# BigBird attention and a low-rank mixer: where the one-hot mask rows and the identity come from, and the order of the first copies

## Chip, cores, metric

The kernel runs on one core of one Trainium2 chip. The metric is the device time of one execution in microseconds (us). Lower is better. A version is timed in several executions, and their median is compared.

The engines have these names in the profile: PE is TensorE (matmul), PEld its weight loads, DVE is VectorE, ACT is ScalarE, POOL is GpSimd, SP is SyncE, which here only issues transfers. A "q" behind the name (SPq, ACTq) is the engine's issue of transfers or its sequencer.

## The reference

Inputs: q, k, v of 4 batches x 8 heads x 768 tokens x 64 channels, a table of 3 sampled key blocks for each of the 24 query blocks (a block has 32 tokens), and the weights U (768x32), V (32x768), w1 (512x2048) and w2 (2048x512) of a mixer. All but the table are float32.

```python
scores = scale * np.matmul(q, k.transpose(0, 1, 3, 2))
mask = np.abs(blk_i - blk_j) <= 1
mask = mask | (blk_i == 0) | (blk_j == 0) | (blk_i == n_blocks - 1) | (blk_j == n_blocks - 1)
for qb in range(n_blocks):
    for kb in sampled_blocks[qb]:
        mask[qb * block:(qb + 1) * block, kb * block:(kb + 1) * block] = True
scores = np.where(mask, scores, -1000000000.0)
scores = scores - np.max(scores, axis=-1, keepdims=True)
attn = np.exp(scores)
attn = attn / (np.sum(attn, axis=-1, keepdims=True) + 1e-09)
attn_out = np.matmul(attn, v)
x = np.ascontiguousarray(attn_out.transpose(0, 2, 1, 3)).reshape(B, S, H * D)
h = x.transpose(0, 2, 1) @ U @ V
u = x + h.transpose(0, 2, 1)
out = u + np.maximum(u @ w_ch1, 0.0) @ w_ch2
```

## The kernel before

**Pairs of heads.** The 32 heads are worked as 16 pairs, four pairs to a batch. For each pair q and k are turned (channels to partitions), scores are made as keys x queries in PSUM, exponentials are taken from there on ScalarE, and the exponentials are the weights of the products with v. In the first batch (pairs 0 to 3) the mask is put into the scores themselves: a head uses 64 partitions for its channels (`drows`), and 24 of the other 64 partitions (`mrows`) for the mask. On the query side (`qres`) these rows hold a one-hot row for each block, on the key side (`kres`) the bias (0 or -240) of each key and block. One matmul over 128 partitions then gives score plus bias. Head 0 of a pair has its channels in partitions 0 to 63 and its mask rows from 64, head 1 the other way round. There are two such sets (`qres[0]`, `kres[0]` and `qres[1]`, `kres[1]`), all four in one tile `res`, used by even and odd pairs. Later batches multiply the exponentials by a mask in SBUF, which `mask_part` (PLAN letter K) makes from `kmask` and the one-hot rows.

**The start (lines 234 to 342).** It is written out by hand, engine by engine. SP issues the loads of q and k of head 0, then the one-hot rows of the first set (`one_hot`, two loads from a constant in memory), then head 1, v and the next pair. ScalarE issues the loads of `small` (a constant of 128 rows with the static mask, the block numbers and the 128x128 identity) and of the table `sb`. VectorE zeroes the unused rows. TensorE does eight matmuls of ones with 512 columns (`keep_warm`, line 272). VectorE casts q of head 0 to float16 (`first_cast`), makes the bias from table and constants (lines 302 to 309), and casts k. The first turns (`first_turn`, line 227) are matmuls of the 64 channels of head 0 with the identity: three to a half of 384 tokens (c), for q (n = 0) and k (n = 1). `first_row` (line 293) copies a half to its rows of the set. `mask_half` (line 279) multiplies the bias by the one-hot rows, into PSUM bank 2 for c = 0 and bank 7 for c = 1, and `mask_row` (line 287) copies 24 rows of it to the mask rows of a head. GpSimd zeroes the second set, writes the column of ones of the v tiles `vts`, casts q and k of head 1, zeroes `Vt` and `kmask` and casts what comes in later. `second_set` copies the mask rows of the first set to the second and to `kmask` by transfers on SP.

**The order behind it.** A string, PLAN (line 448), has a word for each step; the steps are issued in its order, and each engine works on what it is given in that order. A capital letter takes the next step of its kind, a digit behind it is its PSUM bank. S is a score of one block of 128 keys (`score`, line 980), B a score of two (`two_scores`, line 999, three banks from the digit on), e the exponential of the oldest score that has none, Z the turn of q and k of pair 0 for head 1 (`last_turn`, line 352, both heads wide), z its copy (line 359), A a product with v, R the turn of a later pair, K a part of the SBUF mask. It begins:

```
S0 S3 e e S5 B0 e Z7 e S3 z Z6 e z A7 A B0 e R6 S3 t A R5 e A B0 t A K6 e A S3 k v A5 A e K6 k B0 A
```

`begin(i)` runs as the first score of pair i is issued, and issues loads of later pairs (`loads`). S0 uses PSUM banks 0 and 1, S3 banks 3 and 4, S5 banks 5 and 6, B0 banks 0 to 2. The first turns of k are in banks 5 and 6.

## Time and profile before

| what | us |
|---|---|
| three runs | 269.93, 270.38, 272.29 |
| median | 270.38 |
| the profiled execution, whole | 270.01 |
| its span, first to last instruction | 268.2 |
| TensorE at work in the span | 262.4 |
| VectorE | 232.5 |
| ScalarE | 202.7 |
| GpSimd | 72.7 |

The granted TensorE clock is 0.999 in the mean over the span. All times of the trace are counted from the start of the span. Busy times of matmuls hold a modelled drain, so that neighbours overlap in it: the start of the next is the better measure. The profile merges instructions of one line that follow each other into one row, "x8", with the length from the first start to the last end. A row's "[0.22 <-ACT res L287]" says that the engine had been idle for 0.22 us, and what ended that. L293 is line 293 of the listing.

### The profile page before, as it was taken

The numbers are of one execution on the slowest core, as the hardware profiler recorded it, in microseconds if no ns is written. First come the engines' busy times: TensorE is split into PE (matmuls) and PEld (weight loads), VectorE is DVE, ScalarE is ACT, GpSimd is POOL, SyncE is SP. The second block draws the span as 40 slices with busy tenths as digits, with TensorE's granted clock in tenths as the row PEclk, the third lists the DMA queues.
The fourth block names the chain that finished last, engine by engine and source line by source line (L and its number), as shares of the span: only waits on it lengthen the run. The fifth ranks groups of instructions, "written<-read, shape, count | busy, mean of one in ns | idle before, by whom it ended". The sixth has DMA issues, their size and how long they took to land.

```text
span 268.2 us, 7303 instructions
## 1 busy us (share of the span) xinstructions
PE 262.4 (98%) x3006; PEld 182.4 (68%) x3006; DVE 232.5 (87%) x477; ACT 202.7 (76%) x265; POOL 72.7 (27%) x98
## 2 busy tenths in 40 slices
PE   8899999999999999999999999999999999999995
PEld 3677775555577778565666887555667788666884
DVE  5789988988999998868588997688998999999993
ACT  4999998897989667788898857788997944789200
POOL 4669006944462570070606160000000000000000
PEclk9999999999999999999999999999999999999999
DMA  6799997999999999897938997610200116400024
GB/s 192 245 324 263 207 235 123 113 135 144 189 146 133 117 103 111 284 98 89 90 39 67 106 109 139 223 34 13 51 0 2 42 42 117 159 2 0 2 98 137
DMA packets 88720, 31.66 MB, mean 118 GB/s; under 512 B 77104, under 2 KB 85840, under 8 KB 88688
## 3 DMA queue, kind: packets, MB, share of 16 engines
q0 software_dynamic: 49728, 10.10, 48.4%
q1 hardware_dynamic: 38492, 20.86, 33.6%
q8 instruction: 23, 0.38, 0.6%
q10 hardware_dynamic: 468, 0.26, 0.4%
q14 instruction: 9, 0.07, 0.1%
HBM read 27.67 MB, written 6.29 MB: 127 GB/s over the span
## 4 chain that ended last, share of the span: by engine, by line
PE 73%; DMA 12%; DVE 7%; ACT 2%; POOL 2%; issue 1%; SPq 0%; DVEq 0%; POOLq 0%; ACTq 0%
PE ps L760 32%; PE ps L685 17%; DMA w2t<-in_moe_w_ch_dram 9%; PE ps L414 9%; PE ps L1030 7%; DMA vld<-in_v_dram 2%; PE ps L999 2%; ACT est L1007 2%; PE ps L980 1%; DVE est L1045 1%; PE ps L272 1%; DMA qpl<-stqld 1%; PE ps L665 1%; DVE xf L551 1%; DVE res L969 1%
## 5 line engine op out<-in xcount | busy, mean ns | idle before, releaser
L1039 ACT ACTIVATE est<-ps 128x1536 f16<-128x1536 f32 x72 | 100.6, 1450 | 18.8 <-PE ps L1030 18.7
L685 PE MATMUL ps<-uT,w1t 128*128 128x384 f16 x384 | 70.2, 326 | 0.0
L1045 DVE TENSOR_TENSOR est<-est,mask 128x1440 f16<-128x1440 f16 x72 | 63.4, 903 | 0.6 <-ACT est L1039 0.2
L685 PEld LDWEIGHTS <-w1t 128*128 128x128 f16 x384 | 35.6, 97 | 26.6 <-issue 6.8
L414 PEld LDWEIGHTS <-est 128*128 128x128 f16 x1152 | 40.4, 97 | 7.0 <-issue 3.3
L414 PE MATMUL ps<-vt,est 128*128 128x65 f16 x1152 | 43.3, 193 | 0.2 <-DVE xf L551 0.2
L760 PEld LDWEIGHTS <-hid 128*128 128x128 f16 x358 | 34.0, 98 | 6.6 <-issue 1.6
L697 ACT ACTIVATE hid<-ps 128x384 f16<-128x384 f32 x63 | 29.7, 496 | 4.8 <-PE ps L685 4.3
L1030 PE MATMUL ps<-qpl,kpl 64*128 64x512 f16 (+1 forms) x288 | 31.7, 325 | 0.0
L139 POOL DMA_DIRECT2D stqld<-in_q_dram x20 | 16.3, 820 | 55.9 <-DMA qpl<-stqld 54.4
L760 PE MATMUL ps<-w2t,hid 128*128 128x256 f16 x238 | 31.1, 273 | 0.0
L879 DVE TENSOR_TENSOR xf<-xf,ps 128x256 f32<-128x256 f32 x63 | 25.4, 416 | 4.1 <-PE ps L760 3.7
L699 DVE TENSOR_SCALAR hid<-ps 128x384 f16<-128x384 f32 x33 | 18.3, 555 | 8.7 <-PE ps L685 8.0
L760 PEld LDWEIGHTS <-sums 128*128 128x128 f16 x216 | 20.1, 98 | 4.4 <-issue 1.0
L989 ACT ACTIVATE est<-ps 128x768 f16<-128x768 f32 x30 | 22.5, 812 | 0.1
L1030 PEld LDWEIGHTS <-kpl 64*128 64x128 f16 x288 | 12.3, 94 | 14.3 <-issue 9.1
L760 PE MATMUL ps<-res,sums 128*128 128x256 f16 x144 | 19.4, 273 | 0.0
L634 ACT CAST xh<-xf 128x384 f16<-128x384 f32 x24 | 11.0, 510 | 10.0 <-DVE xf L630 10.0
L551 DVE TENSOR_TENSOR xf<-ps,rcp 128x384 f32<-128x384 f32 x32 | 17.7, 554 | 0.8
L139 POOL DMA_DIRECT2D stkld<-in_k_dram x20 | 16.3, 819 | 1.9 <-issue 0.8
L139 POOL DMA_DIRECT2D vt<-in_v_dram x20 | 16.3, 820 | 0.0
L760 PE MATMUL ps<-res,hid 128*128 128x256 f16 x120 | 15.9, 273 | 0.0
(121 smaller groups left out, 339.3 us busy)
## 6 DMA issues: line engine op xcount, KB each, us to landing
out_dram<-xf SPq DMA_DIRECT2D x18, 256.0 KB, 2.4
vld<-in_v_dram SPq DMA_DIRECT2D x6, 384.0 KB, 6.3
w1t<-in_moe_w_ch_dram POOLq DMA_DIRECT2D x4, 512.0 KB, 8.3
w2t<-in_moe_w_ch_dram POOLq DMA_DIRECT2D x4, 512.0 KB, 12.1
qld<-in_q_dram SPq DMA_DIRECT2D x5, 384.0 KB, 3.7
kld<-in_k_dram SPq DMA_DIRECT2D x5, 384.0 KB
stqld<-in_q_dram POOLq DMA_DIRECT2D x20, 96.0 KB, 3.9
stkld<-in_k_dram POOLq DMA_DIRECT2D x20, 96.0 KB, 4.2
```

What stands on the lines that cost most here:

```text
L139: nc.gpsimd.dma_start(out=dst[:, h], in_=src[b, 2 * hp + h].rearrange("(p t) d -> p t d", t=T),)
L414: nc.tensor.matmul(pav[:, sc, :], est[:, n, sc * P : (sc + 1) * P], vts[b % 2][:, 2 * hp + h, g, 0 : D + 1], start=(g == 0 and sc == 0), s ...
L551: nc.vector.tensor_tensor(out=dst, in0=pav[:, :, 0:D], in1=rcp[:, :, None].broadcast_to([P, T, D]), op=ALU.mult,)
L685: nc.tensor.matmul(pt, w1t[:, cc, jj * P : (jj + 1) * P], bts[b].uT[:, cc, c * HS : (c + 1) * HS], start=(cc == 0), stop=(cc == NCC - 1), ...
L697: nc.scalar.activation(out=dst, in_=pt, func=AF.Relu)
L699: nc.vector.tensor_scalar_max(out=dst, in0=pt, scalar1=0.0)
L760: nc.tensor.matmul(acc[key], lhsT, rhs, start=(first and i == 0), stop=(i == len(pairs_) - 1), skip_group_check=True,)
L879: nc.vector.tensor_add(out=x, in0=x, in1=acc[a, b, tau])
L989: lambda: nc.scalar.activation(out=dst, in_=ps, func=AF.Exp, scale=0.125),
L1030: nc.tensor.matmul(units[h][:, u * S + lo : u * S + hi], kT[drows[h], g * P : (g + 1) * P], qT[drows[h], lo:hi], start=True, stop=True, sk ...
L1039: nc.scalar.activation(out=both[h], in_=units[h].rearrange("p (g n) -> p g n", g=2), func=AF.Exp, scale=0.125,)
L1045: lambda: nc.vector.tensor_mul(out=masked(both[h]), in0=masked(both[h]), in1=masked(mask[:, 2 * j : 2 * j + 2, :]),),
```

## The change

- The identity becomes a constant of its own, `id16`, loaded by SP between q and k of head 0.
- One-hot rows, static mask and block numbers become one constant of 32 rows (`hot`), loaded by ScalarE's queue. The load goes to partitions 0 to 31 of `res`, from the query rows of head 1 of the first set on, and 50 elements into the next: the one-hot rows thus land where head 1 of the first set needs them, and the constants in rows of the second set that are filled later.
- Head 0 of the first set gets its one-hot rows (and the zeros below) by a copy on ScalarE, the second set by two transfers inside SBUF (`second_hot`). The four loads of `one_hot` are gone. VectorE zeroes 32 rows of head 1 in the place of 64 of each head.
- The first turns take both heads of the staged tile as weights (128 columns for 64); head 1's half is zeroed by GpSimd before. Their output has 128 partitions, of which 64 are read.
- There are seven warming matmuls of 512 columns and one of 256 in the place of eight.
- The copies are dealt out anew: `first_row(1, 0)` is all VectorE's, `first_row(1, 1)` ScalarE's. The second `mask_half`, and the mask copies but for the first, go to a step of their own, `late_masks`, behind the first score (W7 in PLAN; bank 7), with `second_set` and the load of V.
- GpSimd writes the ones of `vts` and zeroes `kmask` behind its casts of head 1; it zeroes `Ut` (which VectorE did) and `Vt` beside the cast of U. It zeroes only the rows of the second set that no copy fills.
- The loads of pair 2 are issued at the first score of pair 1 in the place of pair 0.

```diff
--- before.py
+++ after.py
@@ -64,14 +64,14 @@
     ).astype(np.float32)
     cols = np.arange(S)
     blk = ((cols % P) * T + cols // P) // BLK
-    ohT_np = (blk[None, :] == ii[:, None]).astype(np.float16)
-    small_np = np.zeros((P, NB + 1 + P // 2), np.float32)
-    small_np[:NB, :NB] = (ms_np - 1.0) * -MASK_BIAS
-    small_np[:NB, NB] = ii
-    small_np[:, NB + 1 :] = np.eye(P, dtype=np.float16).view(np.float32)
-
-    small_dr = nc.inline_tensor(small_np, name="small_const")
-    ohT_dr = nc.inline_tensor(ohT_np, name="one_hot_const")
+    NROW = 32
+    hot_np = np.zeros((NROW, S // 2 + NB + 1), np.float32)
+    hot_np[:NB, : S // 2] = (blk[None, :] == ii[:, None]).astype(np.float16).view(np.float32)
+    hot_np[:NB, S // 2 : S // 2 + NB] = (ms_np - 1.0) * -MASK_BIAS
+    hot_np[:NB, S // 2 + NB] = ii
+
+    hot_dr = nc.inline_tensor(hot_np, name="hot_const")
+    id_dr = nc.inline_tensor(np.eye(P, dtype=np.float16), name="identity_const")
 
     consts = ctx.enter_context(tc.tile_pool(name="consts", bufs=1))
     wpool = ctx.enter_context(tc.tile_pool(name="wpool", bufs=1))
@@ -99,10 +99,7 @@
         ring["psc"] += 1
         return PS[:, (0, 3)[ring["psc"] % 2] :][:, 0:2]
 
-    small = consts.tile([P, NB + 1 + P // 2], FP32)
-    ms = small[0:NB, 0:NB]
-    iota = small[0:NB, NB : NB + 1]
-    id16 = small[:, NB + 1 :].bitcast(FP16)
+    id16 = consts.tile([P, P], FP16, name="id16")
     sb = consts.tile([P, NB, 3, 2], I32)
     vts = [consts.tile([P, H, T, DV], FP16, name=f"vt{i}") for i in range(2)]
     NEST = 16
@@ -112,6 +109,9 @@
     res = consts.tile([P, 4, 2, S], FP16, name="res")
     qres = [res[:, i] for i in range(2)]
     kres = [res[:, 2 + i] for i in range(2)]
+    hot = res.rearrange("p a b s -> p (a b s)")[:, S : 2 * S + 2 * NB + 2].bitcast(FP32)
+    ms = hot[0:NB, S // 2 : S // 2 + NB]
+    iota = hot[0:NB, S // 2 + NB :]
     drows = [slice(0, D), slice(D, P)]
     mrows = [slice(D, D + NB), slice(0, NB)]
     hid = consts.tile([P, 2, 16, HS], FP16, name="hid")
@@ -183,22 +183,24 @@
             out=lds[nm][:, h], in_=src[0, h].rearrange("(p t) d -> p t d", t=T)
         )
 
-    def one_hot(i, h):
-        nc.sync.dma_start(out=qres[i][mrows[h], h, :], in_=ohT_dr.ap())
+    def second_hot(h):
+        nc.sync.dma_start(out=qres[1][mrows[h], h, :], in_=qres[0][mrows[h], h, :])
 
     warm = nc.const_aps.tensor(1.0, [P, 512], mybir.dt.bfloat16)
     bias = consts.tile([P, 2, D], FP16)
 
     def second_set():
         for h in range(2):
-            one_hot(1, h)
             nc.sync.dma_start(out=kres[1][mrows[h], h, :], in_=kres[0][mrows[h], h, :])
-        nc.sync.dma_start(out=kmask[mrows[0], :], in_=kres[0][mrows[0], 0, :])
+            if h == 0:
+                nc.sync.dma_start(out=kmask[mrows[0], :], in_=kres[0][mrows[0], 0, :])
 
     def load_mix_u():
         uld = ldpool.tile([P, T, R], FP32, tag="ldu", name="uld", bufs=1)
         nc.sync.dma_start(out=uld, in_=moe_U.rearrange("(p t) r -> p t r", t=T))
+        nc.gpsimd.memset(Ut.bitcast(FP32), 0.0)
         nc.gpsimd.tensor_copy(out=Ut[:, :, 0:R], in_=uld)
+        nc.gpsimd.memset(Vt.bitcast(FP32), 0.0)
 
     def load_mix_v():
         vld = ldpool.tile([P, 2, T, D], FP32, tag="ldv", name="vld")
@@ -225,8 +227,8 @@
         first_out[n, c] = pt
         for j in range(3):
             nc.tensor.matmul(
-                pt[0:D, j * P : (j + 1) * P],
-                sts[0, ("qld", "kld")[n]][:, 3 * c + j, 0],
+                pt[:, j * P : (j + 1) * P],
+                sts[0, ("qld", "kld")[n]][:, 3 * c + j].rearrange("p h d -> p (h d)"),
                 id16,
                 start=(j == 0), stop=(j == 2), skip_group_check=True,
             )
@@ -241,30 +243,31 @@
         }
     ):
         first_load(0, 0, nc.sync)
+        nc.sync.dma_start(out=id16, in_=id_dr.ap())
         first_load(0, 1, nc.sync)
-        nc.scalar.dma_start(out=small, in_=small_dr.ap())
+        nc.scalar.dma_start(out=hot[0:NROW], in_=hot_dr.ap())
         nc.scalar.dma_start(
             out=sb[0:NB].rearrange("k z r w -> k (z r w)"),
             in_=sampled_blocks.bitcast(I32)
             .rearrange("z r -> (z r)")[None, :]
             .broadcast_to([NB, NB * 6]),
         )
-        for h in (1, 0):
-            nc.vector.memset(qres[0][(slice(D, P), slice(0, D))[h], h, :], 0.0)
-            one_hot(0, h)
+        nc.vector.memset(qres[0][NROW:D, 1, :], 0.0)
         nc.vector.memset(bias, 0.0)
         for h in range(2):
-            nc.vector.memset(kres[0][(slice(D, P), slice(0, D))[h], h, :], 0.0)
+            nc.vector.memset(kres[0][drows[1 - h], h, :], 0.0)
         for n in range(2):
             first_load(1, n, nc.sync)
+        for nm in ("qld", "kld"):
+            nc.gpsimd.memset(sts[0, nm][:, :, 1], 0.0)
         for tile_ in (qres[1], kres[1]):
-            nc.gpsimd.memset(tile_.bitcast(FP32), 0.0)
-        for vt in vts:
-            nc.gpsimd.memset(vt[:, :, :, D : D + 1], 1.0)
+            for h in range(2):
+                nc.gpsimd.memset(tile_[drows[1 - h], h, :].bitcast(FP32), 0.0)
         first = consts.tile([P, 1], FP32)
         nc.scalar.activation(
             out=first, in_=nc.const_aps.tensor(1.0, [P, 1], FP32), func=AF.Exp
         )
+        nc.scalar.copy(out=qres[0][drows[1], 0, :], in_=qres[0][drows[0], 1, :])
         pw = psc2()
 
         def keep_warm(n, cols=512):
@@ -273,7 +276,7 @@
                     pw[:, 0, 0:cols], warm[:, 0:P], warm[:, 0:cols], start=True, stop=True
                 )
 
-        pks = [bank(2, [P, HS], FP32), bank(7, [P, HS], FP32)]
+        pks = [bank(2, [P, HS], FP32)]
 
         def mask_half(c):
             nc.tensor.matmul(
@@ -297,7 +300,8 @@
 
         neq = consts.tile([P, NB, 3], FP32)
         a01 = consts.tile([P, NB], FP32)
-        keep_warm(8)
+        keep_warm(7)
+        keep_warm(1, 256)
         first_cast(0, 0, nc.vector.tensor_copy)
         nc.vector.tensor_tensor(
             out=neq[0:NB], in0=sb[0:NB, :, :, 0],
@@ -318,26 +322,30 @@
         first_cast(0, 1, nc.vector.tensor_copy)
         mask_half(0)
         mask_row(0, 0, nc.vector.tensor_copy, 0, P)
-        mask_row(1, 0, nc.scalar.copy)
         first_turn(1, 0)
         first_row(1, 0, nc.vector.tensor_copy, 0, P)
-        first_row(1, 0, nc.scalar.copy, P, HS)
         mask_row(0, 0, nc.vector.tensor_copy, P, HS)
+        first_row(1, 0, nc.vector.tensor_copy, P, HS)
         first_turn(1, 1)
-        first_row(1, 1, nc.vector.tensor_copy)
-        mask_half(1)
-        mask_row(0, 1, nc.vector.tensor_copy)
-        mask_row(1, 1, nc.vector.tensor_copy)
+        first_row(1, 1, nc.scalar.copy)
 
         for n in range(2):
             first_cast(1, n, nc.gpsimd.tensor_copy)
-        for tile_ in (Vt, kmask):
-            nc.gpsimd.memset(tile_.bitcast(FP32), 0.0)
-        nc.vector.memset(Ut, 0.0)
+        for vt in vts:
+            nc.gpsimd.memset(vt[:, :, :, D : D + 1], 1.0)
+        nc.gpsimd.memset(kmask.bitcast(FP32), 0.0)
         load_v(0)
         load_qk(1)
         load_v(1)
         load_mix_u()
+        for h in range(2):
+            second_hot(h)
+
+    def late_masks(n):
+        pks.append(bank(n, [P, HS], FP32))
+        mask_half(1)
+        for h, c in ((0, 1), (1, 0), (1, 1)):
+            mask_row(h, c, nc.vector.tensor_copy)
         second_set()
         load_mix_v()
 
@@ -446,7 +454,7 @@
 
 
     PLAN = """
-    S0 S3 e e S5 B0 e Z7 e S3 z Z6 e z A7 A B0 e R6 S3 t A R5 e A B0 t A K6 e A S3 k v A5 A e K6 k B0 A
+    S0 W7 S3 e e S5 B0 e Z7 e S3 z Z6 e z A7 A B0 e R6 S3 t A R5 e A B0 t A K6 e A S3 k v A5 A e K6 k B0 A
     A e K7 A K6 k S3 k A K7 e v B0 k S3 e M6 e A5 A m R7 A t B0 K6 R3 e k A A t S6 A e v S0 D2 S3 e d A7
     A e A S0 K6 A e S3 k K2 A e S5 k A e v S3 R2 e S5 t S0 e M7 e S3 m D2 e B5 d A0 D1 e A A d A S3 D2 A
     e d K1 S5 k R7 e S3 t A S1 e v A5 A e A S3 S6 e K2 A e A k A S3 v B0 e K7 M6 e k S3 m X5 K7 e A6 Y k
@@ -1073,7 +1081,7 @@
         elif i == HP + 2:
             for c in range(1, 4):
                 nc.sync.dma_start(out=Vt[c * R : (c + 1) * R], in_=Vt[0:R])
-        for m in {0: (0,), 1: (1, 2), 3: (3,), 4: (4,)}.get(i, ()):
+        for m in {1: (0, 1, 2), 3: (3,), 4: (4,)}.get(i, ()):
             loads(m)
 
     def first_scores():
@@ -1122,6 +1130,7 @@
         "E": ((lambda n, i=i, c=c: pairs[i].sum_only(c, n),) for i, c in each(range(XP, HP), (0, 1))),
         "R": ((turn_qk, i, n) for i, n in each(range(1, HP + 1), (0, 1))),
         "Z": ((last_turn, n) for n in range(2)),
+        "W": ((late_masks,) for _ in range(1)),
         "K": ((mask_part, g, c) for g, c in each(range(T), (0, 1))),
         "P": ((lambda n, jj=jj: w1(0, 0, jj, n, range(2)),) for jj in range(NPART)),
         "C": ((lambda jj=jj: w1(0, 0, jj, ccs=(2, 3)),) for jj in range(NPART)),
```

## The prediction

> **What bounds the kernel now.** I read three things in order: the busy shares on the page, the busy time by stage, and the chain of waits through the first 10.4 us, which is all the change touches. First the page and the table by stage (from:to in us, length, then busy time and count of each engine, granted clock, DMA share, GB/s).
>
> ```profile
> PE 262.4 (98%) x3006; PEld 182.4 (68%) x3006; DVE 232.5 (87%) x477; ACT 202.7 (76%) x265; POOL 72.7 (27%) x98
> ```
>
> ```profile
> 0.00:4.00 4.00, 3.22 (x8) 1.02 (x8) 2.12 (x7) 1.49 (x2) 2.08 (x8) 1.00 0.48 133
> 4.00:8.00 4.00, 3.50 (x22) 1.69 (x22) 2.99 (x9) 3.02 (x7) 1.72 (x4) 1.00 0.88 268
> ```
>
> TensorE is idle 5.8 us of the span (268.2 - 262.4), and 0.78 + 0.50 = 1.28 of them lie in the first 8 us; the first 0.78 is the launch. Work behind the start is therefore nearly a queue that begins when the start lets it: what the start gains or loses is moved to the end almost one for one, and little else can be gained. Now the chain there (start, length, work).
>
> ```profile
> 0.78 3.57 PE ps L272 x8
> 4.35 0.47 PE ps L227 x3
> 4.84 0.85 ACT res L293 x2
> 5.69 0.46 ACT res L287
> 6.17 0.42 DVE res L287
> 6.62 0.55 DVE res L293
> 7.21 0.57 DVE res L287
> 7.82 0.82 PE ps L999 x4
> 8.64 0.34 PE ps L352 x6
> 8.98 0.32 PE ps L980 x2
> 9.30 0.35 PE ps L352 x6
> 9.74 0.57 DVE res L359
> 10.36 0.84 PE ps L999 x4
> ```
>
> Eight warming matmuls hold TensorE to 4.35, then come the turns of the first q, two copies and a mask copy on ScalarE, three copies on VectorE, the fused score B0 at 7.82, and the turns of the second heads with a last copy before the second B0 at 10.36. The timeline of the same stretch gives starts and lengths of single operations.
>
> ```profile
> 0.73 1.41 POOL L261 MEMSET res<- 128x768 f32 x2 [0.29 <-POOLq L1168]
> 1.20 0.41 SPq L182 DMA_DIRECT2D kld<-in_k_dram  x1
> 1.65 0.80 SPq L187 DMA_DIRECT2D res<-one_hot_const  x2
> 3.15 0.20 ACT L265 ACTIVATE first<-const-float32-1.0 128x1 f32<-128x1 f32 x1
> 3.47 0.36 DVE L213 CAST stqld<-qld 128x384 f16<-128x384 f32 x1 [0.52 <-DMA qld<-in_q_dram]
> 4.28 0.60 PEld L227 LDWEIGHTS <-stqld 128*64 128x64 f16 x6 [0.84 <-DVE a L306]
> 4.38 0.34 DVE L213 CAST stkld<-kld 128x384 f16<-128x384 f32 x1
> 5.24 0.52 PE L227 MATMUL ps<-small,stkld 128*64 128x128 f16 x6
> 5.35 0.29 DVE L287 CAST res<-ps 24x128 f16<-24x128 f32 x1 [0.62 <-PE ps L279]
> 5.67 0.28 DVE L293 CAST res<-ps 64x128 f16<-64x128 f32 x1
> 6.17 0.42 DVE L287 CAST res<-ps 24x256 f16<-24x256 f32 x1 [0.22 <-ACT res L287]
> 6.54 2.23 ACT L989 ACTIVATE est<-ps 128x768 f16<-128x768 f32 x3
> 6.74 0.81 PE L980 MATMUL ps<-res 128*128 128x384 f16 x4 [0.23 <-DVE res L287]
> 7.21 1.13 DVE L287 CAST res<-ps 24x384 f16<-24x384 f32 x2
> 8.41 0.82 POOL L131 CAST vt<-vld 128x768 f16<-128x768 f32 x1 [0.90 <-DMA vld<-in_v_dram]
> 8.68 1.45 ACT L1007 ACTIVATE est<-ps 128x1536 f16<-128x1536 f32 x1
> 13.89 1.55 POOL L207 CAST Vt<-vld 32x768 f16<-32x768 f32 x1 [0.56 <-DMA vld<-in_moe_V_dram]
> ```
>
> **The change, part by part.**
>
> *Half a warming matmul less.* Eight took 3.57 us, 0.446 each, so TensorE is free 0.22 us sooner. The q cast is done at 3.47 + 0.36 = 3.83, so the turn can use that time.
>
> *Wide turns.* Weights of 128 columns replace weights of 64, the moving side stays 128 columns. The rows of weight loads and matmuls (min/median/max ns) are:
>
> ```profile
> L227 PEld LDWEIGHTS <-stqld x6: 128/175/177, 4.3 to 4.7; 128*64 128x64 f16 x6
> L227 PE MATMUL ps<-small,stqld x6: 234/314/316, 4.3 to 4.8; 128*64 128x128 f16 x6
> L352 PEld LDWEIGHTS <-stqld x6: 96/98/98, 8.3 to 8.7; 128*128 128x128 f16 x6
> L227 PE MATMUL ps<-small,stkld x6: 217/218/243, 5.2 to 5.5; 128*64 128x128 f16 x6
> ```
>
> A wide load at full speed takes 98 ns, and in the chain its turns (8.64, six in 0.34) load ahead of the matmul before. The narrow loads began only at 4.28, as the last warming matmul drained, 0.45 us after their cast. I take a further 0.06 us from loading ahead (between 0 and 0.13, to which the cast's end limits it). The first turn starts 0.28 us sooner, about 4.07 in the chain's times. The Trainium skill, page "TensorE: Matmul & The Clock Gate", section "LDWEIGHTS (loading the stationary operand)", speaks against this: a load costs its columns over 1.2 GHz whatever its rows, so a wide one would be twice a narrow one, 107 against 53 ns, and twelve turns would lose up to 0.6 us if nothing hid it. The rows here say otherwise (98 ns for 128 columns), and the rows decide.
>
> *The constants.* The identity leaves ScalarE's DMA and gets its own on SP, ahead of the k load, whose issue slips by one issue, about 0.4 us (k's here takes 0.41). The mask constants and the one-hot rows come in one load on ScalarE's queue; two one-hot issues (0.80 us) leave SP, so everything behind k on SP goes about 0.4 sooner. In 2.8 to 3.2 us the DMA view has these rows, and the k load its time to landing:
>
> ```profile
> q10 hardware_dynamic: 26, 0.01, 8.3%
> ```
>
> ```profile
> kld<-in_k_dram SPq DMA_DIRECT2D x1, 192.0 KB, 2.9
> ```
>
> The first is ScalarE's queue, which moves its last packets there, so the constants are in by about 3.2 and should be in the new form too. k lands at 1.20 + 2.9 = 4.1 and will at about 4.5; its cast, at 4.38 now, slips to about 4.55 and ends near 4.9, and the k turn that stood at 5.24 can start near 4.95. That is 0.29 sooner, just the lead. The cover here is thin: each tenth by which k lands after 4.55 is lost.
>
> *ScalarE's copy of the one-hot rows.* Nearest row: the three exponentials of 768 columns, 2.23 us, 0.74 each. Behind the first activation (ends 3.35) it ends at 4.1. ScalarE's next work stood at 4.84 and comes at about 4.56. Cost nothing; if the constants came at 4.0, 0.2 us would be lost.
>
> *GpSimd.* Two memsets of the staged tiles (half of res's 0.70 each at most) go ahead of the turns, done by about 1.5. The zeroing of Ut and Vt, some 0.4 us each, now stands between the second v cast and Vt's cast, where GpSimd waited 0.56 for a DMA; the earlier loads give the rest. The ones column and kmask follow the second heads' casts, before v at 8.41, which waited 0.90 for its DMA. Cost nothing; without that cover, 0.3 us of GpSimd time, not on the chain. loads(0) is moved behind the late masks' SP transfers, where those stood before, so no queue order changes there.
>
> *The copies.* This is where the lead is spent. ScalarE loses a mask copy (0.46) and a k copy and gains the last k copy (row L293); VectorE loses that and gains the k copy of 256 columns (0.42, as the mask copy of that width) and a mask copy (0.57), and its wait of 0.22 on ScalarE goes. From starts to starts: the first mask copy 5.35 becomes 5.07, then 0.32, 0.31, 0.45 and 0.45, so the four rows are in by 6.57 where they were by 6.59. The second score, at 6.74, gains 0.02. The three late mask copies at 0.58 each start at 6.60, 7.18 and 7.76 and end at 8.31; the last ended at 7.21 + 1.13 = 8.34. The late mask matmul stands between the first and second score, where TensorE waits anyway.
>
> *What is late next.* The first exponential comes 0.28 sooner (6.26), the second only 0.02 to 0.04, as its scores wait for VectorE; the fourth, B0's, follows the third on ScalarE at 8.66 against 8.68. B0 itself no longer waits at 7.82: three of its matmuls need the first late copy and the fourth the second (bank 2), 7.75, so it ends near 8.15 in place of 8.64. The turn Z7 then waits for the third (bank 7), 8.31, and starts at about 8.37, against 8.48 for its weight-ahead start; the chain has it after B0 at 8.64, so the lead is between 0.11 and 0.27. I take 0.11, the timing of its start. Z7, a score, Z6, the copy and the second B0 follow unchanged: 10.36 becomes 10.25, and the exponential behind it has ScalarE free by then (8.66 + 1.45 = 10.11, then a single one). **Sum: 0.1 us sooner**, with 0.0 and 0.28 as bounds.
>
> **To the time measured.** The profiled execution took 270.01 (span 268.2); less 0.11 is 269.90. The three runs have 269.93, 270.38 and 272.29, median 270.38; less 0.11 is 270.27. The profiled one lies 0.37 under the median, and I take halfway: 270.1.
>
> **The rivals.**
>
> *The clock stays low.* The q turns took 316 ns, the last of them 234, the k turns 218: TensorE's clock rose at about 4.7, after 3.9 us of matmuls without a gap. With half a matmul less a gap can open, if the identity, now behind q on SP, lands after 4.1. If the clock then stays low for another such stretch, the work up to 8.2 us doubles: two mask products and three pairs of scores of 384 columns, B0 and the k turns, by the chain's rows 0.32 a pair and 0.82 for B0, some 2.4 us, less the 0.50 idle: +1.9, so 272.2. Against it: q lands at 3.4, the identity is a sixth of its bytes just behind, and a gap of a tenth is small. Decided by whether TensorE idles by more than a few tenths before 4.7. Chance 0.08. The skill's page named above, Part 1, has the clock wait for a busy window of 3.4 us that runs freely; seven and a half warming matmuls at 0.446 are 3.35, just less, but the turns behind them are matmuls too; the rise after 3.9 us here agrees with such a window and cannot show where it begins.
>
> *No gain.* k lands after 4.8, or VectorE's new copies cost 0.1 more: 270.4 to 270.7. For it: VectorE has no idle time left between 5.1 and 8.3. Chance 0.25.
>
> *More gain.* The lead of the first turn, 0.28, survives, and the earlier loads take up the remaining gaps to 16 us (0.2 or so each): 0.5 to 0.8 sooner, 269.5. Against it: VectorE. Chance 0.14.
>
> *Later transfers collide.* Loads go 0.4 us sooner, and TensorE later works from weights that arrive by DMA; a slip there of 3 us would pass to the end. Nothing in the first 16 us says that it will: 273 and over. Chance 0.04.
>
> The forecast keeps 0.49. The range reaches from 269.2 (more gain, and the 0.3 by which runs differ) to 271.4 (no gain, the same added to the runs above the median), and leaves out the low clock and the collision. Over 1% is 2.7 us, about what a measurement of this kernel can tell from no change; only the collision gets there, and nothing shown saves as much: faster 0.02, within 0.94, slower 0.04.
>
> **What would show it.** Right: the first turn's weight load near 4.0 with q turns at about 315 ns and k turns at 218; the first exponential near 6.25 but the second still near 7.2; VectorE without a gap from 5.1 to 8.3; Z7 near 8.4 and the second B0 near 10.25; from 24 us the same pattern, shifted. Wrong: matmuls of 300 ns behind 5 us (clock), a k cast after 4.8, a ScalarE copy that ends after 4.5, or a shift at 16 us that the end does not have.

## The result and the profile after

| | before | after |
|---|---|---|
| median of 22 executions each, us | 270.38 | 272.12 |
| lowest and highest, us | 269.65, 272.29 | 270.59, 273.86 |
| profiled execution, us (span) | 270.01 (268.2) | 270.59 (268.8) |
| ratio after/before, 95% interval | | 1.0057 (1.0040 to 1.0073) |

The changed kernel is slower by 0.6%, less than the 1% that counts as a change here, but outside the range of the prediction. Two numbers have to be explained: the profiled executions differ by only 0.6 us, the medians by 1.7. Of the 22 times after, 7 lie from 270.59 to 271.48 and 15 from 271.82 up; of those before, 20 lie at 270.94 or below. The profiled execution after is the fastest of its 22, so it shows what the fastest execution loses, and not what is lost most of the time.

The page of after, and its table by stage for the first 8 us (from:to, length, busy time and count of PE, PEld, DVE, ACT, POOL, granted clock, DMA share, GB/s):

```profile
PE 262.0 (97%) x3006; PEld 182.3 (68%) x3006; DVE 232.3 (86%) x476; ACT 203.4 (76%) x265; POOL 74.1 (28%) x103
```

```profile
0.00:4.00 4.00, 3.21 (x10) 1.15 (x11) 1.82 (x7) 2.12 (x3) 2.62 (x10) 1.00 0.46 114
4.00:8.00 4.00, 2.97 (x22) 1.45 (x21) 3.08 (x9) 2.77 (x6) 1.80 (x5) 1.00 0.91 279
```

From 4 to 8 us TensorE now works 2.97 us where it worked 3.50. The timeline of after there (start, length, work, and the idle time before it with what ended it):

```profile
1.21 0.41 SPq L246 DMA_DIRECT2D id<-identity_const  x1
1.66 0.43 SPq L182 DMA_DIRECT2D kld<-in_k_dram  x1
...
3.37 0.83 ACT L270 COPY res<-res 64x768 f16<-64x768 f16 x1
...
3.87 0.35 PEld L229 LDWEIGHTS <-stqld 128*128 128x128 f16 x6 [0.43 <-POOL res L265]
3.90 0.49 PE L229 MATMUL ps<-id,stqld 128*128 128x128 f16 x6
...
4.92 0.36 DVE L215 CAST stkld<-kld 128x384 f16<-128x384 f32 x1 [0.56 <-DMA kld<-in_k_dram]
...
5.43 0.49 PE L229 MATMUL ps<-id,stkld 128*128 128x128 f16 x6 [0.68 <-DVE stkld L215]
...
6.67 2.40 ACT L997 ACTIVATE est<-ps 128x768 f16<-128x768 f32 x3 [0.24 <-PE ps L988]
...
6.99 1.60 DVE L290 CAST res<-ps 24x384 f16<-24x384 f32 x3
...
8.64 0.50 PE L360 MATMUL ps<-id,stqld 128*128 128x128 f16 x6
...
9.79 0.54 PE L422 MATMUL ps<-vt,est 128*128 128x65 f16 x12
...
10.52 0.82 PE L1007 MATMUL ps<-res 128*128 128x512 f16 x4 [0.19 <-DVE res L367]
```

The q turns start 0.4 us sooner than before (weight load 3.87 for 4.28), and at 218 ns a turn they run at full speed at once. Then TensorE stands idle for 0.68 us, because k of head 0 is not there: VectorE itself waits 0.56 for the transfer and casts k at 4.92, where it did at 4.38. The k turns come at 5.43 for 5.24, the second B0 at 10.52 for 10.36. The first product with v starts at 9.79; before it was here:

```profile
9.63 0.54 PE L414 MATMUL ps<-vt,est 128*128 128x65 f16 x12
```

So the start loses 0.16 us. The second loss is far behind the change, at 30 us. The timeline of VectorE and TensorE there, after:

```profile
29.09 0.55 DVE L624 TENSOR_TENSOR xf<-xf,ps 128x384 f32<-128x384 f32 x1
...
29.97 0.48 PE L988 MATMUL ps<-res 128*128 128x384 f16 x2
...
30.09 0.55 DVE L623 TENSOR_TENSOR xh<-xh,ps 128x384 f16<-128x384 f16 x1 [0.45 <-issue]
...
31.16 0.32 PE L947 MATMUL ps<-res,kmask 128*128 128x384 f16 x1 [0.35 <-DVE xf L624]
...
31.98 0.49 PE L988 MATMUL ps<-res 128*128 128x384 f16 x2
```

And the same sum of VectorE and the same two scores of TensorE before:

```profile
29.52 0.56 DVE L615 TENSOR_TENSOR xh<-xh,ps 128x384 f16<-128x384 f16 x1
...
29.81 0.48 PE L980 MATMUL ps<-res 128*128 128x384 f16 x2
...
31.43 0.48 PE L980 MATMUL ps<-res 128*128 128x384 f16 x2
```

VectorE stops for 0.45 us ahead of the third of the low-rank sums (the steps D of PLAN), and nothing that the profile shows is being waited for ("issue"). TensorE waits 0.35 for it. The distance between the kernels, 29.97 - 29.81 = 0.16 ahead of it, is 31.98 - 31.43 = 0.55 behind it. The profiled executions end 0.58 us apart, so these two places are nearly all of that difference. The other 1.2 us of the medians are not in this trace.

### The profile page after: what moved, and what is told of

Same layout as the page of the kernel before. It is cut to its first block, busy times and chain, and to the rows that moved or that the text cites. A ratio compares the mean times of both kernels' runs of the same rounds, so it can differ in the third digit from the quotient of the medians.

```text
span 268.8 us, 7310 instructions
## 1 busy us (share of the span) xinstructions
PE 262.0 (97%) x3006; PEld 182.3 (68%) x3006; DVE 232.3 (86%) x476; ACT 203.4 (76%) x265; POOL 74.1 (28%) x103
## 4 chain that ended last, share of the span: by engine, by line
PE 66%; DMA 10%; DVE 7%; POOL 3%; issue 1%; ACT 1%; DVEq 0%; POOLq 0%; ACTq 0%
PE ps L768 31%; PE ps L693 17%; PE ps L422 7%; PE ps L1038 7%; DMA stqld<-in_q_dram 5%; DMA vt<-in_v_dram 4%; PE ps L988 1%; DVE est L1053 1%; POOL stkld L139 1%; DMA qpl<-stqld 1%; DVE xf L887 1%; POOL stqld L139 1%; DVE sums L863 1%; DVE sums L729 1%; DVE xf L559 1%
```

## The experiments

Each kernel was executed 6 to 12 times and timed against the kernel before on the same chip; ratios are to that, as recorded. They are not the quotients of the medians of all executions (for six warming matmuls these medians, 270.82 and 270.19, give 1.0023). "Lowest" is the distance of its fastest execution from the fastest of the kernel before on that chip.

| kernel | ratio (95% interval) | lowest, us |
|---|---|---|
| after again | 1.0055 (1.0028 to 1.0082) | +0.84 |
| k ahead of the identity | 1.0053 (1.0017 to 1.0090) | +0.78 |
| three matmuls in the gap | 1.0067 (1.0033 to 1.0101) | +1.20 |
| before, 7.5 warming matmuls | 0.9999 (0.9967 to 1.0032) | -0.16 |
| identity on ScalarE's queue | 1.0088 (1.0066 to 1.0110) | +1.64 |
| the same, one more zeroing | 1.0115 (1.0092 to 1.0137) | +2.72 |
| after, one more zeroing | 1.0044 (1.0020 to 1.0067) | +0.59 |
| before, a transfer ahead of k | 1.0043 (1.0014 to 1.0072) | +0.20 |
| after, constants as before | 1.0025 (1.0006 to 1.0044) | +0.65 |
| before, six warming matmuls | 1.0000 (0.9979 to 1.0021) | -0.33 |
| one matmul in the gap | 1.0035 (1.0014 to 1.0056) | +0.96 |
| before, wide turns and 7.5 | 1.0010 (0.9981 to 1.0040) | -0.39 |
| before, two zeroings moved | 0.9977 (0.9951 to 1.0002) | +0.40 |
| constants as before, one more zeroing | 1.0010 (0.9972 to 1.0048) | +0.11 |
| before, four warming matmuls | 1.0048 (1.0019 to 1.0076) | +1.54 |
| identity on GpSimd's queue | 1.0015 (0.9983 to 1.0047) | +0.87 |
| two zeroings moved, again | 1.0001 (0.9986 to 1.0017) | +0.60 |
| its twin with one more | 0.9994 (0.9973 to 1.0015) | +0.45 |

### The changed kernel once more

> The changed kernel, unchanged, for the trace of another of its executions. In the one profiled, k's cast waits for its load until 4.92 us and TensorE is idle for most of 4.7 to 5.4; its 270.59 us is the fastest of 22 runs, whose median is 272.12. Theory K (late k load: the identity's transfer on SP ahead of k holds up the k turns, nothing else): this trace looks like the first, and the ratio to before is 1.002 to 1.004. Theory C (clock: the idle stretch keeps TensorE's clock low for longer in most executions, so that the start costs 1 to 2 us there): matmuls behind 5.4 us take about 0.31 us for 128 columns in place of 0.22, the second fused score starts at 11.5 or later (10.52 in the first trace), ratio 1.005 to 1.007. Theory L (later transfers): the start as in the first trace, the time is lost behind 16 us.

It came out as the first time, 1.0055. Its profiled execution took 271.74 and is one of the slower kind. Its timeline:

```profile
3.93 0.84 PE L229 MATMUL ps<-id,stqld 128*128 128x128 f16 x6
...
5.68 0.80 PE L229 MATMUL ps<-id,stkld 128*128 128x128 f16 x6 [0.48 <-DVE stkld L215]
...
7.72 1.46 PE L988 MATMUL ps<-res 128*128 128x384 f16 x4
...
9.85 0.50 PE L360 MATMUL ps<-id,stqld 128*128 128x128 f16 x6
...
11.01 0.54 PE L422 MATMUL ps<-vt,est 128*128 128x65 f16 x12
```

Six turns last 0.84 and 0.80 where they lasted 0.49, and 0.50 again from 9.85 on. TensorE's clock rose at 9.43 us here; in the first profiled execution it rose at 3.50. (Each trace's record of the granted clock begins at that rise. Ahead of it the column of the tables by stage reads 1.00 though the matmuls are slow, so a first rise is told by the durations of equal matmuls, not by that column.) The first product with v starts at 11.01 for 9.79, 1.22 later, and the execution is 271.74 - 270.59 = 1.15 longer. This is a part of the loss that the first trace doesn't show.

The lateness of k varies too. In the five traces that have the identity ahead of k, its cast starts at 4.92, 5.17, 5.30, 5.33 and 5.50: the first trace is the mildest.

### Half a warming matmul less, alone

```diff
-        keep_warm(8)
+        keep_warm(7)
+        keep_warm(1, 256)
```

> The kernel before with seven and a half warming matmuls in place of eight and nothing else. The prediction: up to 0.2 us faster, ratio 0.999 to 1.000. Theory C with the shorter warming as its cause: ratio 1.003 or more, q turns at 314 ns and k turns no faster.

The ratio is 0.9999 (to 1.0032): no cost of this part is measured. Its profiled execution is instructive all the same:

```profile
5.27 0.85 PE L227 MATMUL ps<-small,stkld 128*64 128x128 f16 x6
...
6.48 2.10 PE L981 MATMUL ps<-res 128*128 128x384 f16 x6
...
11.01 0.54 PE L415 MATMUL ps<-vt,est 128*128 128x65 f16 x12
```

No idle time stands before the k turns, and the clock rose late here too, at 10.07. So a late rise also comes with k in time. What a gap could change is how often.

### Where the identity is fetched

Three kernels move the one transfer that the change put ahead of k. First, behind k on SP's queue:

```diff
-        nc.sync.dma_start(out=id16, in_=id_dr.ap())
         first_load(0, 1, nc.sync)
+        nc.sync.dma_start(out=id16, in_=id_dr.ap())
```

> The changed kernel with the identity's load issued behind k's in place of ahead of it. Theory K: k's cast goes back to about 4.4, the turns of k to 4.9, unless the turns of q now wait for the identity (it lands at about 4.1 then); ratio to before 0.999 to 1.000. Theory C: the idle stretch is gone as well, so the same ratio, and the spread of the runs falls from over 3 us to about that of before. Theory L: ratio stays at 1.004 to 1.007.

Nothing is won, 1.0053. The gap only moves ahead of the q turns, which need the identity (the profiled execution ran at a mean granted clock of 0.951 and took 278.23, so only the order of its timeline is read):

```profile
4.91 0.80 PE L229 MATMUL ps<-id,stqld 128*128 128x128 f16 x6 [0.77 <-DMA id<-identity_const]
```

Second, ahead of the constants and the table on ScalarE's queue, without and with one more zeroing of VectorE:

```diff
-        nc.sync.dma_start(out=id16, in_=id_dr.ap())
         first_load(0, 1, nc.sync)
+        nc.scalar.dma_start(out=id16, in_=id_dr.ap())
         nc.scalar.dma_start(out=hot[0:NROW], in_=hot_dr.ap())
```

> The changed kernel with the identity's load on ScalarE's queue, ahead of the constants, so that SP issues q and k one behind the other as before. Theory G (gap: TensorE waits between the first mask matmul and the turns of k, because k's load is issued 0.45 us later; that alone also makes its clock rise late in more executions): k's cast back at about 4.4, no gap, ratio to before 1.000 to 1.002, with most runs within 1 us of the fastest. Theory W (the other parts of the start, wide turns and new order of copies, cost the time): ratio stays 1.004 to 1.007.

> The same with one more VectorE instruction early (a second zeroing of the bias, 0.11 us, where VectorE waits for data anyway). In all traces of the changed kernel VectorE stands still for 0.45 us at about 30 us, in front of the third sum of the low-rank part, waiting for nothing that the profile shows, and TensorE then waits 0.35 us for it; in no trace of the kernel before. Theory I (the stall hangs on the place of that instruction in VectorE's stream, which the change moved by one): the stall is gone, 0.3 to 0.4 us less than the run without it, ratio to before 0.998 to 1.001. Theory X (the stall comes from transfers or GpSimd): it stays.

Both are worse than the change, 1.0088 and 1.0115. The load of k takes 2.8 us again, but the table `sb`, now third on its queue, is late. VectorE waits for it, comes to the cast of k only at 5.45, and the gap moves to the mask product (lines of the first of the two):

```profile
4.81 0.22 DVE L306 TENSOR_TENSOR neq<-sb,res 24x72 f32<-24x72 int32 x1 [1.06 <-DMA sb<-in_sampled_blocks_dram]
...
5.57 0.33 PE L282 MATMUL ps<-res,bias 24*128 24x384 f16 x1 [0.80 <-DVE bias L313]
```

The additional zeroing took the stall at 30 us away, but not the time that was expected to go with it. In that trace the clock, up at 4.71, is down again from 8.12 to 11.54.

Third, on GpSimd's queue, which is empty then:

```diff
-        nc.sync.dma_start(out=id16, in_=id_dr.ap())
+        nc.gpsimd.dma_start(out=id16, in_=id_dr.ap())
```

> The changed kernel with the identity fetched on GpSimd's queue, so that nothing stands between q and k on SyncE's; VectorE's and ScalarE's streams stay as they are, so the stall at 30 us stays too. Theory A (the identity ahead of k is what delays k): k lands by 4.2 us, no gap over 0.3 us before its turns, and the loss shrinks to that of the stall, 1.0005 to 1.003, provided the identity lands by 3.9; if it lands later, the gap shows before the turns of q and 1.004 to 1.007 is left. Theory B (k is late because of the number of bytes in flight or for another reason): k lands at 4.7 or later in spite of it, and 1.005 to 1.007.

The list of transfers (KB each, us from issue to landing) and the timeline:

```profile
kld<-in_k_dram SPq DMA_DIRECT2D x2, 192.0 KB, 2.9
...
id<-identity_const POOLq DMA_DIRECT2D x1, 32.0 KB, 3.6
```

```profile
4.39 0.49 DVE L215 CAST stkld<-kld 128x384 f16<-128x384 f32 x1
...
4.88 0.49 PE L229 MATMUL ps<-id,stqld 128*128 128x128 f16 x6 [1.00 <-DVE stkld L215]
```

k takes 2.9 us again and is cast at 4.39 without a wait: the identity ahead of it was what delayed it. But the identity, issued at 1.22, lands 3.6 later, and now the q turns wait for it. (The row names the k cast as releaser, which came just before; the turn of q doesn't read it, and 1.22 + 3.6 is 4.82.) The ratio, 1.0015, is not told apart from 1 nor from 1.004.

The table by stage of this execution shows that a gap can also take the clock down again (the granted clock stands ahead of the last two columns):

```profile
4.00:6.90 2.90, 1.76 (x16) 1.01 (x16) 1.98 (x7) 1.55 (x5) 1.20 (x4) 1.00 0.87 227
6.90:10.30 3.40, 3.34 (x15) 1.74 (x15) 1.82 (x4) 2.60 (x4) 2.34 (x6) 0.50 1.02 353
10.30:14.00 3.70, 3.51 (x53) 2.71 (x52) 2.00 (x4) 3.08 (x3) 2.94 (x6) 1.00 0.44 100
```

The clock rose at 3.50 here, as in the first trace of the change. There a gap of 0.68 us followed and the clock stayed up; here a gap of 1.00 us followed, and it was at a half from 6.91 to 10.32, for 3.41 us (one execution each). This lowers the mean granted clock of the whole execution to 0.993. Of the 22 executions of the change seven have 0.993 or 0.994, all of them among the 15 slower ones; of the 138 executions of the kernel before beside these experiments one has. So in seven of the 15 the loss came with a fall of the clock. For the other eight the mean doesn't tell: the late first rises at 9.43 and 10.07 left it at 0.998 and 1.000.

### A transfer ahead of k in the kernel before

The kernel before, with an additional load of 32 KB between q and k that nobody reads (its constant and its tile are declared further up, not shown):

```diff
         first_load(0, 0, nc.sync)
+        nc.sync.dma_start(out=spare16, in_=id_dr.ap())
         first_load(0, 1, nc.sync)
```

> The kernel before with a transfer of 32 KB that nobody reads between the loads of q and k on SP: only k comes later, all else is the old order, narrow turns and eight warming matmuls. Theory G: a gap of 0.3 to 0.7 us in front of the turns of k, later clock in more executions, ratio 1.003 to 1.006. Theory W: no more than the wait itself, ratio 1.000 to 1.002.

1.0043: one small transfer makes most of the loss. Its list of transfers and its timeline:

```profile
kld<-in_k_dram SPq DMA_DIRECT2D x1, 192.0 KB, 3.5
```

```profile
5.23 0.36 DVE L215 CAST stkld<-kld 128x384 f16<-128x384 f32 x1 [0.73 <-DMA kld<-in_k_dram]
...
5.83 0.85 PE L229 MATMUL ps<-small,stkld 128*64 128x128 f16 x6
```

k is issued 0.46 later and then takes 3.5 for 2.9 us: some 1.0 in all, and its cast comes 0.85 later. Two of its nine times (269.96 and 270.28) show nothing of it, seven lie from 271.53 to 272.58. In the profiled one of these, 271.58, the k turns last 0.85, the clock rises at 9.85, and the first product with v starts at 11.19, which is 1.56 later than before and more than the lateness of k.

### Filling the gap

Warming matmuls ahead of the k turns of the changed kernel, three of them or one:

```diff
         mask_row(0, 0, nc.vector.tensor_copy, 0, P)
+        keep_warm(3)
         first_turn(1, 0)
```

> The changed kernel with three more warming matmuls of 512 columns between the first mask matmul and the turns of k, where TensorE waits for k's cast: k stays late, TensorE does not idle. Theory K: no gain, ratio 1.003 to 1.008 (the fillers can only be in the way). Theory C: the clock rises as early as before in every execution, ratio 1.000 to 1.002. Theory L: 1.004 to 1.007.

> The changed kernel with one more warming matmul (512 columns) ahead of the turns of k, in the gap of 0.5 us in which TensorE waits for k. Theory A (the gap is what delays the clock): the filler covers most of the gap and the time comes down to about 1.002 to 1.003, the later k and the stall at 30 us being left. Theory B (the gap does nothing to the clock, the lateness of k is all): 1.0055 as without it, or more, since a filler at the low clock lasts longer than the gap and pushes the turns of k back.

Three are too many: in the profiled execution they last 1.36 us at the low clock and push the k turns to 6.33 (1.0067). One brings 1.0035, with 10 of 12 times below 271.9 where the change had 8 of 22. But the intervals of the two overlap, and in its profiled execution a gap of 0.27 us is left and the clock rises only at 9.92. This doesn't settle whether the gap or the lateness costs more.

### A gap with no late load

The kernel before with six, and with four, warming matmuls:

```diff
-        keep_warm(8)
+        keep_warm(6)
```

> The kernel before with six warming matmuls for eight: TensorE stands idle for about 0.4 us before the turns of q, and no load is late. Theory A (an idle gap of TensorE before 5 us lets the granted clock rise one window later in most executions, whatever makes the gap): 1.002 to 1.005, with single times on two levels about 1 us apart, and matmuls of the turns and scores at their long durations until 9 us in the profiled execution when it is on the upper level. Theory B (only the later data costs, the gap does nothing to the clock): 0.999 to 1.0005, because the q turns wait for the same load as before.

> The kernel before with four warming matmuls for eight: TensorE stands idle for more than 1 us before the turns of q, while no load and no copy is late. Theory A (an idle gap of TensorE in its first 5 us delays the rise of its clock): nearly all single times lie on the upper level, about 271 to 272, and the profiled execution has matmuls at their long durations until 9 us or beyond; 1.003 to 1.006. Theory B (the gap by itself does nothing): 0.999 to 1.001, because the turns start when the cast of q ends, as before.

Six make a gap of 0.34 us ahead of the q turns, and the ratio, 1.0000, shows no loss, where the theory of the clock had expected 1.002 to 1.005. Its profiled execution has a late rise all the same, at 8.69 us, with the first product with v at 10.22 for 9.63:

```profile
6.26 2.10 PE L980 MATMUL ps<-res 128*128 128x384 f16 x6
```

So whether a gap of that size does harm stays open. Four make one of 1.21 us, and all 12 times lie at 271.11 or above, the lowest 1.54 above that of the kernel before; the ratio is 1.0048. The timeline of the kernel with four:

```profile
3.85 0.85 PE L227 MATMUL ps<-small,stqld 128*64 128x128 f16 x6 [1.21 <-DVE stqld L213]
...
6.70 2.10 PE L980 MATMUL ps<-res 128*128 128x384 f16 x6
...
9.88 0.85 PE L352 MATMUL ps<-small,stqld 128*128 128x128 f16 x6
...
11.79 0.57 PE L414 MATMUL ps<-vt,est 128*128 128x65 f16 x12
```

The q turns start no later than before (weight load at 4.28 there), and still the first product with v comes 2.16 later than in the profiled execution before, since turns last 0.85 until beyond 11 us; the clock rises at 11.87. One load, of the one-hot rows, was late in this execution, by 0.39, too little for that. An idle TensorE in its first microseconds can by itself put the rise off.

**A loss that is not at the start.** That execution took 274.21, and 1.8 us of its loss lie between 65 and 84 us. The longest wait of VectorE there, 1.4 us, is for a load of the mixer's weights. The same wait stands in the trace of the change with one more zeroing (272.42); the first line is its, the second that of the kernel before:

```profile
76.62 0.69 DVE L730 TENSOR_TENSOR w2t<-w2t 128x1024 f16<-128x1024 f16 x1 [1.64 <-DMA w2t<-in_moe_w_ch_dram]
```

```profile
74.63 0.69 DVE L721 TENSOR_TENSOR w2t<-w2t 128x1024 f16<-128x1024 f16 x1 [0.24 <-DMA w2t<-in_moe_w_ch_dram]
```

There the clock rose at 5.42 and the first product with v came at 10.18; a score at 74.36 is 0.59 behind the kernel before (73.77), a product with v at 81.72 is 1.99 behind (79.73). A third trace, of the kernel before with two zeroings moved (the second time), has the wait too. In the kernel with three matmuls in the gap TensorE waits 1.4 us for another transfer at 170 us. So a slow execution is not always one with a late clock, and a single time doesn't say which it is. What makes these loads late was not tried.

### The other parts

The wide turns with 7.5 warming matmuls, in the kernel before (the edit of the warming matmuls, as above, and GpSimd's zeroing of head 1's half are not shown):

```diff
-                pt[0:D, j * P : (j + 1) * P],
-                sts[0, ("qld", "kld")[n]][:, 3 * c + j, 0],
+                pt[:, j * P : (j + 1) * P],
+                sts[0, ("qld", "kld")[n]][:, 3 * c + j].rearrange("p h d -> p (h d)"),
```

> The kernel before with the wide turns of the first heads and 7.5 warming matmuls, its constants untouched. Theory A (these two parts cost nothing): 0.997 to 1.001, the first turn at about 4.0 us, no gap over 0.3 us before the turns of k. Theory B (the wide turns cost by their longer weight loads, or the shorter warming opens a gap that the clock answers): 1.002 to 1.005.

1.0010, with the fastest time of all, 269.43. The lead of the first turn is real in the trace (3.93 for 4.28), but it is gone by the first product with v (9.66 for 9.63), and it doesn't move the median.

The whole change with the constants laid out as before:

```diff
-        nc.sync.dma_start(out=id16, in_=id_dr.ap())
         first_load(0, 1, nc.sync)
-        nc.scalar.dma_start(out=hot[0:NROW], in_=hot_dr.ap())
+        nc.scalar.dma_start(out=small, in_=small_dr.ap())
...
-        nc.vector.memset(qres[0][NROW:D, 1, :], 0.0)
+        for h in (1, 0):
+            nc.vector.memset(qres[0][drows[1 - h], h, :], 0.0)
+            nc.sync.dma_start(out=qres[0][mrows[h], h, :], in_=ohT_dr.ap())
...
-        nc.scalar.copy(out=qres[0][drows[1], 0, :], in_=qres[0][drows[0], 1, :])
```

> The changed kernel with the constants laid out as before: mask constants and identity together on ScalarE's queue, both one-hot loads on SyncE's queue behind q and k, no identity ahead of k and no one-hot copy on ScalarE; the wide turns and the 7.5 warming matmuls stay. Theory A (all of the loss comes with the place of the constants: k lands 0.5 to 0.8 us later, and the stall of 0.45 us of VectorE at 30 us comes with the number of instructions ahead of it there): k lands by 4.1 again, TensorE has no gap over 0.3 us between 4 and 5.4 us, VectorE runs from the first mask copy on without the stall at 30 us, and the time is 0.997 to 1.001 of the kernel before. Theory B (the wide turns or the shorter warming cost something by themselves): 1.003 to 1.006.

Its timeline:

```profile
4.23 0.34 DVE L215 CAST stkld<-kld 128x384 f16<-128x384 f32 x1
...
5.13 0.77 PE L229 MATMUL ps<-small,stkld 128*128 128x128 f16 x6
...
29.96 0.55 DVE L623 TENSOR_TENSOR xh<-xh,ps 128x384 f16<-128x384 f16 x1 [0.45 <-issue]
```

k is in time, no gap is left, and 10 of 12 times lie between 270.47 and 271.31: the slower kind has become rare in this series. (The same kernel with one more zeroing, below, has six of 12 times at 271.27 or above, on a chip where the kernel before has 15 of 35 at 271.20 or above. The share is not a matter of the kernel alone.) What is left, 1.0025, is on the lowest time too (+0.65), and the trace has the stall at 30 us. That stall was expected to go, since one instruction was back on VectorE; it stayed.

### The stall at 30 us

One more zeroing at the start of VectorE, in the changed kernel and in the one with the old constants:

```diff
         nc.vector.memset(bias, 0.0)
+        nc.vector.memset(bias, 0.0)
```

> The changed kernel with the one more VectorE instruction alone. Theory I: the stall at 30 us is gone, the gap in front of the turns of k is there, ratio to before 1.003 to 1.006, 0.3 to 0.4 us below the changed kernel. Theory X: stall and ratio as in the changed kernel.

> The changed kernel with its constants laid out as before (as in the run before this one) and one more zeroing instruction of VectorE at the start, which puts 62 ahead of the third low-rank sum. Theory A (place of the instruction): no stall at 30 us, and 0.4 us less than 270.99, so 0.999 to 1.0015 of the kernel before. Theory B (the stall has nothing to do with the count): stall and time as without it, 1.002 to 1.003.

In both the stall is gone. What counts is not the instructions alone but also the additional ones that wait (an instruction that waits for more than one semaphore has a record EVENT_SEMAPHORE beside it). Counted together, 61 stand ahead of the third low-rank sum in the change (54 and 7), and 61 in the kernel with the old constants (55 and 6), which is why one more didn't help there. Of the 20 traces of this study, the 10 with 61 have the stall, the 10 with 62 or 63 have none. The test was to make 61 of them in the kernel before, which has 63, by giving two zeroings to GpSimd:

```diff
         for h in (1, 0):
-            nc.vector.memset(qres[0][(slice(D, P), slice(0, D))[h], h, :], 0.0)
+            nc.gpsimd.memset(qres[0][(slice(D, P), slice(0, D))[h], h, :].bitcast(FP32), 0.0)
```

> The kernel before with two of VectorE's zeroing instructions at the start (the first head's zeros in the padded q) given to GpSimd; nothing else moves. Theory A (the stall of 0.45 us of VectorE at 30 us comes from the place of the third low-rank sum in VectorE's stream: every traced kernel in which 61 instructions and extra semaphore waits stand ahead of it has the stall, every one with 62 or 63 has none; here it would be 61): the stall of 0.45 us appears in a kernel without any part of the change, and the time is 1.001 to 1.0025 of the kernel before. Theory B (the stall belongs to the changed data flow, its loads or its turns): no stall, 0.999 to 1.0005.

The stall came, in a kernel without any of the change. Its timeline:

```profile
30.02 0.55 DVE L615 TENSOR_TENSOR xh<-xh,ps 128x384 f16<-128x384 f16 x1 [0.45 <-issue]
```

The time expected with it did not: 0.9977, within noise of 1, with a lowest time 0.40 above that of the kernel before and few of the slower kind. In the profiled execution the stall is handed on: TensorE is 0.09 behind the kernel before at the first product with v (9.72) and at 29.90, 0.48 behind at 31.91, and the execution ends 0.38 later. Two runs more were to price the stall, the same kernel and its twin with one zeroing added:

> The kernel before with two of VectorE's zeroing instructions given to GpSimd, once more, beside its twin of the next run on the same chip. It has the stall of 0.45 us at 30 us (61 ahead of the third low-rank sum). Theory A (the stall is passed on to the end): its fastest single times lie 0.3 to 0.45 us above those of the twin. Theory B (the stall is absorbed later): the same fastest times within 0.1.

> The same with one more zeroing instruction on VectorE at the start, 62 ahead of the third low-rank sum: no stall. Theory A: fastest single times 0.3 to 0.45 us below the twin's, and a median of 0.997 to 1.000 of the kernel before, which would make it the fastest of all. Theory B: times as the twin's.

The lowest times are 0.15 apart and the medians 270.56 and 270.48, less than the 0.3 expected. The comparison is spoilt by the start: in the twin's trace the mask product waits for the one-hot rows,

```profile
5.36 0.32 PE L280 MATMUL ps<-res,bias 24*128 24x384 f16 x1 [0.67 <-DMA res<-one_hot_const]
```

where the other has no such wait. So the price of the stall rests on the traces, 0.39 us handed to TensorE at 31 us in the change and in the kernel before with two zeroings moved, and on the old constants with and without it: lowest times 0.65 and 0.11 above the kernel before. That it is as much in the median is not shown. No version beat the kernel before by more than its interval.

## Why the prediction was wrong

**Right.** TensorE works as a queue behind the start: the 0.16 lost at the first product is still 0.16 at 29.8 us. The q turns start 0.4 sooner (0.28 forecast), wide loads cost nothing that could be measured (95 to 98 ns each, where the narrow ones for k took 106 to 110 before), ScalarE's copy ends at 4.20 and delays nothing, and VectorE spends the lead on the copies: the three late ones are its last work before Z7, at 8.64.

**The step that failed.** "k lands at 1.20 + 2.9 = 4.1 and will at about 4.5; its cast, at 4.38 now, slips to about 4.55". It slipped to 4.92 in the fastest execution and to 5.17 to 5.50 in four other traces. The issue came 0.46 later, as forecast; the transfer itself took longer, 3.5 for 2.9 us where an unread transfer of the same size was put ahead of k. The step kept the landing time of a kernel that had nothing between q and k. The text had called the cover thin, each tenth behind 4.55 being lost, and then took the one landing time without a margin. So TensorE, which the sum had at the k turns by 4.95, stands idle for 0.68 us and starts them at 5.43: the start loses 0.16 where the sum gained 0.11. The rival "No gain" (k after 4.8, 270.4 to 270.7, chance 0.25) describes this fastest execution, 270.59. It does not describe the median, for the range left out what a gap does to the clock.

**The rival that was right.** The low clock had a chance of 0.08 and a price of 272.2; the median is 272.12. Its mechanism holds (a gap of TensorE, then matmuls at their long durations for several us), its place was wrong: the gap is not at the q turns, for the identity came in time, but at the k turns. That its price meets the median is partly luck: it counted 1.9 us of slow matmuls alone, while in the trace with the late rise the start loses 1.38 (11.01 for 9.63) and the stall, which no step had, adds 0.39. And it was weighed as one event that happens or not. It is a share of the executions: 15 of 22 after lie at 271.82 or above, 2 of 22 before at 271.4 or above. So the median moves by more than the fastest execution, which loses 0.9 (270.59 for 269.65). The share before is not fixed either, as the 15 of 35 on another chip show. One more hint was in the times shown, 269.93 and 272.29 for one kernel, which the prediction read as noise; what made the 272.29 is not shown. The Trainium skill, page "TensorE: Matmul & The Clock Gate", Part 1, has the clock wait for a busy window of 3.4 us that runs freely. The traces agree: the rises at 3.50 us in one execution, 9.43 and 10.07 in others and 11.87 with four warming matmuls fit windows that don't start with the kernel, and the fall of the clock lasted 3.41 us.

**What no step had.** The stall of 0.45 us at 30 us. Nothing of the change touches that place; it moved because VectorE got shorter by an instruction and a wait at the start. "Wrong: ... a shift at 16 us that the end does not have" was the nearest thing that the prediction looked for.

Open stays what VectorE waits for in the stall, and how the slower executions split between the gap, the lateness of k itself and late loads further on. The gap of four warming matmuls shows that a gap suffices; that of six leaves open what a third of a microsecond does. The late loads of the weights are near the rival "Later transfers collide" (chance 0.04), but two of the three traces that have them are of the kernel before with a small edit at its start, so they are not shown to be the change's.

## What to carry to other kernels

A small transfer put ahead of a large one can delay it by more than its own issue, here by 1.0 us for 32 KB. Where a step's cover is a few tenths, leave a margin for that. None of the three other places that were tried for the small one was shown to be better: on each queue something else came late. Price a gap of TensorE in the first 5 us by what it does to the share of executions with a late rise of the clock, and read the single times, not the median alone. When a stall appears far from the change with nothing to wait for, count the engine's instructions ahead of it and try one more.

## What was not expected of the hardware

The rise of TensorE's clock varies between executions of one kernel: 3.50 or 9.43 us in two traces of the change, worth 1.2 us at the end, while the granted clock of the tables reads 1.00 throughout, since its record begins at the rise. Once up, the clock can fall again: with the same rise at 3.50 it stayed up behind a gap of 0.68 us, and was at a half for 3.41 us behind one of 1.00 us, in one execution each.

VectorE's stall of 0.45 us goes with its position: with 61 instructions and waits ahead it is there in 10 of 10 traces, with 62 or 63 in none of 10. The list of DMA queues has a trace of it. From 28 to 32 us the kernel before has an instruction transfer,

```profile
q14 instruction: 1, 0.01, 0.5%
```

and the change has none in that window, but one of the same size between 32 and 36 us. In all 20 traces the first such transfer comes at 28.5 to 31.5 us where there is no stall, and at 33.1 to 35.2 us where there is one. So the fetch of further instructions comes at another point in the kernels that stall. Whether the stall is a wait for instructions was not tried.
